# Input layer of batches 1 to 3 as seven half-size products, gated by Silu in one stretch per batch, and twelve output pairs

## The chip, the core and the metric

The kernel runs on one core of a Trainium2 chip, in one launch. The core's engines work from queues of their own and hand over by semaphores: TensorE (PE) multiplies and writes PSUM, VectorE (DVE) and ScalarE (ACT) read PSUM and SBUF, GpSimd (POOL) works in SBUF, SyncE (SP) issues most DMAs. The metric is the device time of one execution, in microseconds; lower is better.

## What is computed

Attention over 4 batches of 8 heads, 768 tokens and 64 dimensions, in which a query sees only the keys that the centroids assign to its own cluster, then two layers with a gate over 3072 tokens (512 to 2048 to 512).

```python
q_assign = np.argmax(np.einsum('bhsd,hcd->bhsc', q_n, c_n), axis=-1)
k_assign = np.argmax(np.einsum('bhsd,hcd->bhsc', k_n, c_n), axis=-1)
mask = q_assign[:, :, :, None] == k_assign[:, :, None, :]
scores = np.where(mask, scale * np.matmul(q, k.transpose(0, 1, 3, 2)), -1000000000.0)
...
attn = attn / (np.sum(attn, axis=-1, keepdims=True) + 1e-09)
x = np.matmul(attn, v).transpose(0, 2, 1, 3).reshape(B * S, H * D)
h = x @ w_in
g = h * (1.0 / (1.0 + np.exp(-h)))
out = g @ w_out
```

## The kernel before

Every instruction's place is set by hand: `plan` is a list of words, each word is one step, and each engine runs its share of the steps in that order. A word is an operation, a number, and where needed an engine (A for ACT, P for POOL, D for DVE) or a PSUM bank (0 to 3).

*Attention.* A job (`k0` to `k7`, `x0`, `x1`, `h8` to `h31`) is a head's query and key tiles: loaded (`r`), split into two fp16 parts (`hi`, `lo`), transposed (`tr`, `ht`). `L` or `l` multiplies them with the centroids (24 narrow matmuls or 12 wider ones, then `ls`, a sum on DVE); `mx` and `ge` make one-hot rows, which go back beside the tiles (`ct`, `cm`, `ce`; for later jobs `cs`, `cx`, `cv`) so that the score matmul masks itself. A unit is a head, a half of the tokens and 256 keys; there are 192. `qk` makes its scores (two matmuls of 384 columns into a PSUM tile of two banks, L325), `ex` their exponentials (L330), `pv` multiplies those of two heads with the values (36 matmuls of 65 columns, L342), `nm` divides (L352, L354), and `pt`, `pe` or `xd` put the transposed result into `xt`, a tile for each batch and token half.

*Input layer and gate.* For a batch, a token half and a block of 128 of the 2048 features, `e` (with `a`) multiplies four blocks of `w_in` with `xt` (four matmuls of 384 columns, L390). `t` takes tanh(h/2) on ACT (L402), `g` forms (tanh + 1) h on DVE (L405) into `gt`. There are 128 such units, and their words stand spread between the words of the attention of the next batch. One factor 0.5 is applied at the end.

*Output layer.* The six token tiles of a batch form three pairs, (0, 1), (2, 5) and (3, 4). A pair does the two-by-two product of half blocks with seven products (`m1` to `m7`, eight matmuls of 256 columns each, L477) in place of eight: `S1` to `S4` are sums of `gt` on DVE (L490) into `gt` itself or into three tiles, `wc` sums of `w_out` made once, and `z` and `o` take partial results out of PSUM (L499, L505, L508). In `m127` the pair is 12 and the product 7. The pair (0, 1) of batch 0 is left out: its tiles are plain products, `b` (16 matmuls of 512 columns each, L417), with `bo`. The output goes in rows of 512 columns, in the last batch in halves.

The order runs like this: the jobs and attention of batch 0, its input layer beside the attention of batch 1, its output pairs beside that too, and so on; at the end the input layer and the pairs of batch 3. PSUM has eight banks: four by name, and two tiles of two banks each for the scores.

Of the kernel before, what the change touches and what calls it, by code (L numbers as in the profile page):

```python
# [29 lines left out]
def kernel(  # L30
# [42 lines left out]
    zz = const.tile([128, 512], f16, name="zz")  # L73
# [52 lines left out]
    def tr(job, banks, parts="kq"):  # L126
        hl = hls[job.name]
        if job.name not in abs_:
            abs_[job.name] = mp.tile([128, 12, 128], f16, name="ab", bufs=12)
# [43 lines left out]

    def ohv(job):
# [13 lines left out]
    def ge_n(job):  # L188
        m = (job.n + 1) // 2
        nn[job.name] = len(nn)  # L190
# [15 lines left out]
    def c_xpose(job):  # L206
        cd = cds[job.name] = mp.tile([128, 2, 128], f16, name="cdt", bufs=4)
# [52 lines left out]
    vts, vns = {}, {}  # L260

    def load_v(i, eng=nc.sync):
        vn = mp.tile([128, NJ, D], f32, name="vn", bufs=5)
# [3 lines left out]
    def cast_v(i, eng=None):  # L267
# [5 lines left out]
        vts[i] = vt  # L273

# [53 lines left out]
    def exp(u):  # L328
        P = mp.tile([128, 2, HALF], f16, name="P", bufs=13)
# [46 lines left out]
    def xn_d(i, c):  # L376
        b = i // H
        if (b, c) not in xts:
            xts[b, c] = mp.tile([128, NR, HALF], f16, name="xt", bufs=3)
# [20 lines left out]
    def tanh(b, c, fb):  # L400
        tn = tns[b, c, fb] = mp.tile([128, HALF], f32, name="tn", bufs=3)
        nc.scalar.activation(out=tn, in_=phs[b, c, fb][:, 0:HALF], func=AF.Tanh, bias=0.0, scale=0.5)  # L402
# [7 lines left out]
    pos = {}  # L410

    def part_b(b, c, t, n, bk):
        if n == 0:
            pos[b, c, t] = bank("po", bk)
        po = pos[b, c, t]
# [3 lines left out]
    def part_out(b, c, t):  # L419
        j = c * NM + t  # L420
        ot = mp.tile([128, DM], f32, name="ot", bufs=4)
# [408 lines left out]
```

## Time and profile before

| What | Value |
| --- | --- |
| median of 3 runs | 298.83 us |
| lowest and highest | 298.75 and 300.07 us |
| profiled execution, first to last instruction | 297.9 us |
| matmuls of the input layer (L390) | 512, 96.1 us busy |
| matmuls of the output pairs (L477) | 616 |
| exp on ACT (L330) | 192, 151.0 us busy |
| tanh on ACT (L402) | 128, 61.6 us busy |
| gate on DVE (L405) | 128, 68.2 us busy |
| table loads on ACT | 1 |

The page gives the profiled execution by its span alone. In it, "busy" is the time in which at least one instruction of the engine or group ran; matmuls overlap each other, so the busy time of a group of them is more than its share of PE's time.

### The profile page before, as it was taken

How to read it: one execution, taken by the hardware profiler on the slowest of the kernel's cores; microseconds unless marked ns; L12 is line 12 of the kernel's file. 1: busy time of each engine (PE TensorE's matmuls, PEld its weight loads, DVE VectorE, ACT ScalarE, POOL GpSimd, SP SyncE). 2: the span in 40 equal slices, each digit the busy share in tenths (PEclk: the TensorE clock that was granted, in tenths of full speed). 3: DMA queues.
4: the chain of work that ended last, by engine and by line, in shares of the span. 5: the costliest groups of instructions: out<-in, count | busy, mean ns of one | idle time of the engine just before them, and what ended most of it. 6: DMA issues, size and time to landing. Idle time of an engine off the chain costs nothing.

```text
span 297.9 us, 8577 instructions
## 1 busy us (share of the span) xinstructions
PE 288.7 (97%) x3433; PEld 212.6 (71%) x3433; DVE 223.8 (75%) x489; ACT 233.2 (78%) x406; POOL 68.7 (23%) x124
## 2 busy tenths in 40 slices
PE   7899999999979999999999999999999999999995
PEld 3767766666658887777866887767867886777684
DVE  5898849689979986989467897788656733666663
ACT  5998999965979878999789876898669768964731
POOL 2655804000227001334444024220420000000000
PEclk9999999999999999999999999999999999999999
DMA  6999999999997899795399535867221102211103
GB/s 214 286 256 247 179 201 176 193 247 216 171 300 178 171 176 257 176 151 131 102 202 213 164 66 114 256 165 113 51 89 35 26 2 74 82 29 35 39 19 125
DMA packets 75208, 44.13 MB, mean 148 GB/s; under 512 B 54288, under 2 KB 70960, under 8 KB 75168
## 3 DMA queue, kind: packets, MB, share of 16 engines
q1 hardware_dynamic: 70272, 35.75, 50.3%
q0 software_dynamic: 4608, 7.54, 13.5%
q8 instruction: 27, 0.44, 0.6%
q10 hardware_dynamic: 288, 0.30, 0.3%
q14 instruction: 13, 0.11, 0.1%
HBM read 27.30 MB, written 6.29 MB: 113 GB/s over the span
## 4 chain that ended last, share of the span: by engine, by line
PE 87%; DMA 5%; ACT 3%; DVE 3%; issue 1%; SPq 0%; ACTq 0%
PE ph L390 25%; PE pS L325 20%; PE xb L477 18%; PE pO L342 12%; PE psN L159 4%; PE yb L477 3%; PE po L417 2%; DMA ab<-cd 2%; DMA ab<-hl 1%; DMA raw<-in_q_dram 1%; DVE hl L112 1%; PE wb L477 1%; ACT P L330 1%; ACT hl L103 1%; PE pTq L135 1%
## 5 line engine op out<-in xcount | busy, mean ns | idle before, releaser
L330 ACT ACTIVATE P<-pS 128x768 f16<-128x768 f32 x192 | 151.0, 815 | 18.8 <-PE pS L325 17.4
L390 PE MATMUL ph<-xt,win_s 128*128 128x384 f16 x512 | 96.1, 326 | 0.0
L405 DVE SCALAR_TENSOR_TENSOR gt<-tn,ph 128x384 f16<-128x384 f32 x128 | 68.2, 549 | 31.9 <-ACT tn L402 31.0
L325 PE MATMUL pS<-ab 128*128 128x384 f16 x384 | 86.7, 326 | 2.2 <-DMA ab<-cd 1.6
L402 ACT ACTIVATE tn<-ph 128x384 f32<-128x384 f32 x128 | 61.6, 499 | 13.9 <-PE ph L390 10.5
L390 PEld LDWEIGHTS <-win_s 128*128 128x128 f16 x512 | 49.4, 98 | 31.0 <-issue 0.3
L325 PEld LDWEIGHTS <-ab 128*128 128x128 f16 x384 | 34.2, 98 | 18.3 <-DMA ab<-cd 2.2
L342 PEld LDWEIGHTS <-P 128*128 128x128 f16 x1152 | 39.8, 97 | 3.8 <-DVE cd L234 0.4
L342 PE MATMUL pO<-vt,P 128*128 128x65 f16 x1152 | 41.2, 193 | 0.0
L477 PEld LDWEIGHTS <-gt 128*128 128x128 f16 x352 | 34.1, 98 | 6.5
L112 DVE SCALAR_TENSOR_TENSOR hl<-raw,hl 128x768 f16<-128x768 f32 (+3 forms) x35 | 32.0, 916 | 0.8 <-ACT hl L103 0.5
L105 POOL TENSOR_SCALAR hl<-raw 128x768 f16<-128x768 f32 (+1 forms) x9 | 19.5, 2167 | 47.2 <-DVE gt L405 30.7
L477 PEld LDWEIGHTS <-s 128*128 128x128 f16 x264 | 25.5, 98 | 4.7
L199 POOL TENSOR_SCALAR od<-od 128x96 f16<-128x96 f16 x16 | 8.4, 526 | 63.3 <-DVE od L192 63.2
L499 ACT ACTIVATE ot<-xb 128x256 f32<-128x256 f32 x33 | 12.7, 385 | 12.9 <-PE xb L477 12.6
L477 PE MATMUL xb<-wout_s,gt 128*128 128x256 f16 x176 | 22.6, 273 | 0.0
L159 PEld LDWEIGHTS <-ab 128*128 128x128 f16 x544 | 18.9, 97 | 4.1 <-DMA ab<-hl 0.5
L477 PE MATMUL xb<-wc,s 128*128 128x256 f16 x160 | 20.7, 272 | 0.0
L159 PE MATMUL psN<-stk,ab 128*128 128x16 f16 (+1 forms) x544 | 20.1, 184 | 0.1
L354 DVE TENSOR_TENSOR xn<-pO,zr 128x384 f16<-128x384 f32 x32 | 17.8, 557 | 1.1
L490 DVE TENSOR_TENSOR s<-gt 128x1024 f16<-128x1024 f16 x22 | 15.5, 712 | 1.3 <-PE xb L477 1.0
L212 POOL DMA_DIRECT2D ab<-cdt x16 | 9.0, 564 | 19.8 <-PE pS L325 5.2
(93 smaller groups left out, 258.2 us busy)
## 6 DMA issues: line engine op xcount, KB each, us to landing
raw<-in_k_dram SPq DMA_DIRECT2D x31, 192.0 KB, 3.9
raw<-in_q_dram SPq DMA_DIRECT2D x24, 192.0 KB, 3.5
out_dram<-ot SPq DMA_DIRECT2D x18, 256.0 KB, 2.9
vn<-in_v_dram SPq DMA_DIRECT2D x19, 192.0 KB, 4.7
vn<-in_v_dram POOLq DMA_DIRECT2D x13, 192.0 KB, 3.4
win_s<-in_moe_w_in_dram POOLq DMA_DIRECT2D x8, 256.0 KB, 6.8
wout_s<-in_moe_w_out_dram POOLq DMA_DIRECT2D x4, 512.0 KB, 9.2
out_dram<-ot SPq DMA_DIRECT2D x12, 128.0 KB, 1.8
```

The costliest lines, as they stand in the source:

```text
L105: nc.gpsimd.tensor_scalar(out=o, in0=i, scalar1=QS, scalar2=None, op0=ALU.mult)
L112: nc.vector.scalar_tensor_tensor(out=hl[:, s, 1, :], in0=raws[job.name][:, s, :], scalar=QS, in1=hl[:, s, 0, :], op0=ALU.mult, op1=ALU.sub ...
L159: nc.tensor.matmul(L[:, n % 2, :, n // 2], ab[:, i, :], stk[:, job.groups[i // 3][0], x : x + w], start=(x == 0), stop=(x + w == 2 * HC),)
L325: nc.tensor.matmul(pS[:, e, 0:HALF], abs_[kj.name][:, kn, :], rhs, start=True, stop=True)
L330: nc.scalar.activation(out=P, in_=pst.pop(u)[:, :, 0:HALF], func=AF.Exp, bias=0.0, scale=ESC)
L342: nc.tensor.matmul(o[:, (2 * t + h) * VW : (2 * t + h + 1) * VW], Ps[i + h, c, j // 2][:, j % 2, ts(t, 128)], vtb[(i + h) % 13][:, j, 0:VW ...
L354: nc.vector.tensor_tensor(out=xn, in0=ov[:, :, 0:D], in1=zr.unsqueeze(2).to_broadcast([128, 2 * NM, D]), op=ALU.mult)
L390: nc.tensor.matmul(ph[:, 0:HALF], win_s[:, r, ts(fb, 128)], xts[b, c][:, r, :], start=(r == 0), stop=(r == NR - 1))
L402: nc.scalar.activation(out=tn, in_=phs[b, c, fb][:, 0:HALF], func=AF.Tanh, bias=0.0, scale=0.5)
L405: nc.vector.scalar_tensor_tensor(out=gt[:, fb, NM * c : NM * c + NM, :].rearrange("p t n -> p (t n)"), in0=tns.pop((b, c, fb)), scalar=1.0 ...
L477: nc.tensor.matmul(o, self.lhs(l, f), self.rhs(r, f), start=(f == 0 and opens), stop=(f == HB - 1), skip_group_check=True)
L490: nc.vector.tensor_tensor(out=o, in0=a, in1=b_, op=op)
```

## The change

*Input layer of batches 1 to 3.* The two-by-two product is used here as well: the blocks are the two halves of the 512 inputs, the two halves of the 2048 features and the two halves of the tokens. A group `g` of eight covers 128 features of each half. `y` is one of its seven products (two matmuls of 384 columns), with the number batch, group, product: `y107` is batch 1, group 2, product 7. `ws` makes the sums of `w_in` once, `T` the sums of `xt` for each batch. Products 7, 2 and 4 add up in one bank (`gy`, or one half of `gd`), products 1, 6, 3 and 5 in another (`gx`, or the other half). Between the products the partial sums are joined: `u0` copies the bank of product 7 to `sb`, `u1` copies the bank of product 1 into it, `u2` and `u3` add `sb`. `s0` to `s3` are the gates of the four blocks, each one Silu on ACT into `gt`. Batch 0 keeps `e`, `t` and `g`.

*Stretches.* The words of a batch's input layer stand together, with few others between them, and the 48 units of the next batch come behind. One exp, `ex102`, stands within the first stretch.

*Output.* Pair (0, 1) of batch 0 is `Pair` number 11, so there are twelve pairs and no plain tiles. The values' column of ones is 2.0, which halves x; with that the factor 0.5 at the end and in the tanh goes, and Silu takes a scale of 2. Sums `S2` and `S4` go into `gt` in place, one tile `s3` is left, sums can be on POOL, copies from PSUM on DVE or ACT. Each half row is stored by itself.

*Places.* Score tiles have fixed banks (`d4`, `d5`), which the groups use as well. Some pools are smaller, `zz` lies in `s3`, `ohm` in `ohd`. Jobs 8, 10, 11 and 14 use `l` where they had `L`. The units' order within a batch is another one.

```diff
@@
-    ohm = [const.tile([128, 2 * HC * 6], f16, name=f"om{n}") for n in range(3)]
     ohd = [const.tile([128, 2, 128], f16, name=f"od{n}") for n in range(3)]
+    ohm = [t.rearrange("p h n -> p (h n)")[:, 0 : 2 * HC * 6] for t in ohd]
...
-            abs_[job.name] = mp.tile([128, 12, 128], f16, name="ab", bufs=12)
+            abs_[job.name] = mp.tile([128, 12, 128], f16, name="ab", bufs=10)
...
-        cd = mp.tile([6 * HC, 256], f16, name="cd", bufs=4)
+        cd = mp.tile([6 * HC, 256], f16, name="cd", bufs=3)
...
-    def qk_mm(u):
-        if u >= NU:
-            return
+    def double(name, n):
+        return ps.tile([128, 2, 512], f32, name=name, tag=f"d{n}", bufs=1)
+
+    def qk_mm(u, bk):
         i, c, m = units[u]
-        pS = ps.tile([128, 2, 512], f32, name="pS", tag="st", bufs=2)
+        pS = double("pS", bk)
...
-        P = mp.tile([128, 2, HALF], f16, name="P", bufs=13)
+        P = mp.tile([128, 2, HALF], f16, name="P", bufs=12)
...
-            xts[b, c] = mp.tile([128, NR, HALF], f16, name="xt", bufs=3)
+            xts[b, c] = mp.tile([128, NR, HALF], f16, name="xt", bufs=2)
...
-        tn = tns[b, c, fb] = mp.tile([128, HALF], f32, name="tn", bufs=3)
-        nc.scalar.activation(out=tn, in_=phs[b, c, fb][:, 0:HALF], func=AF.Tanh, bias=0.0, scale=0.5)
+        tn = tns[b, c, fb] = mp.tile([128, HALF], f32, name="tn", tag="tn", bufs=5)
+        nc.scalar.activation(out=tn, in_=phs[b, c, fb][:, 0:HALF], func=AF.Tanh, bias=0.0, scale=1.0)
...
-    def part_b(b, c, t, n, bk):
...
-        for fc in range(4 * n, 4 * n + 4):
-            nc.tensor.matmul(po, gt[:, fc, NM * c + t, :], wout_s[:, fc, :], start=(fc == 0), stop=(fc == NFB - 1))
...
+    def w_sum(g, k, eng):
+        s2, s3_, s4 = (ws[:, n, :, 256 * g : 256 * g + 256] for n in range(3))
+        o, a, b_, op = (
+            (s3_, w_half(0, 0, g), w_half(1, 0, g), ALU.subtract),
+            (w_half(1, 0, g), w_half(1, 0, g), w_half(1, 1, g), ALU.add),
+            (s2, w_half(1, 0, g), w_half(0, 0, g), ALU.subtract),
+            (s4, w_half(0, 1, g), s2, ALU.subtract),
+        )[k]
+        eng.tensor_tensor(out=o, in0=a, in1=b_, op=op)
...
+    def x_sum(b, k, eng):
...
+            (t3, x_half(b, 1, 1), x_half(b, 0, 1), ALU.subtract),
+            (x_half(b, 0, 1), x_half(b, 0, 1), x_half(b, 0, 0), ALU.subtract),
+            (t2, x_half(b, 1, 1), x_half(b, 0, 1), ALU.subtract),
+            (t4, x_half(b, 1, 0), t2, ALU.subtract),
...
+    def group_mm(b, g, s, bk):
+        if s in (7, 1):
+            if s == 7 and bk > 3:
+                o = double("gd", bk)
+                ys[b, g, 7], ys[b, g, 1] = o[:, 0, :], o[:, 1, :]
+            elif (b, g, s) not in ys:
+                ys[b, g, s] = bank("gy" if s == 7 else "gx", bk)
+        o = ys[b, g, 7 if s in (7, 2, 4) else 1]
...
+        for r in range(2):
+            nc.tensor.matmul(
+                o[:, 0:HALF], w[:, r, :], x[:, r, :], start=(s in (7, 1) and r == 0), stop=(r == 1), skip_group_check=True
+            )
+
+    def group_mix(b, g, k, eng):
+        y = ys[b, g, 7][:, 0:HALF]
+        if k == 0:
+            sbs[b, g] = mp.tile([128, HALF], f32, name="sb", tag="tn", bufs=5)
+        sb = sbs[b, g]
+        if k < 2:
+            o, i = (y, ys[b, g, 1][:, 0:HALF]) if k else (sb, y)
+            if eng == "D":
+                nc.vector.tensor_copy(o, i)
+            else:
+                nc.scalar.activation(out=o, in_=i, func=AF.Copy, bias=0.0, scale=1.0)
+        else:
+            x = ys[b, g, 1][:, 0:HALF]
+            nc.vector.tensor_tensor(out=(y, sb)[k - 2], in0=x, in1=sb, op=ALU.add)
...
+    def group_silu(b, g, j):
+        i, o = group_h(b, g, j)
+        nc.scalar.activation(out=o, in_=i, func=AF.Silu, bias=0.0, scale=2.0)
...
-                "S3": (sums["S3"], a11, a21, ALU.subtract),
+                "S3": (s3, a11, a21, ALU.subtract),
                 "S1": (a21, a21, a22, ALU.add),
-                "S2": (sums["S2"], a21, a11, ALU.subtract),
-                "S4": (sums["S4"], a12, sums["S2"], ALU.subtract),
+                "S2": (a11, a21, a11, ALU.subtract),
+                "S4": (a12, a12, a11, ALU.subtract),
             }[name]
-            nc.vector.tensor_tensor(out=o, in0=a, in1=b_, op=op)
+            eng.tensor_tensor(out=o, in0=a, in1=b_, op=op)
...
-    duos = [Pair(b, x, y) for b in range(B) for x, y in ((0, 1), (2, 5), (3, 4)) if (b, x) != (0, 0)]
+    duos = [Pair(b, x, y) for b in range(B) for x, y in ((0, 1), (2, 5), (3, 4)) if (b, x) != (0, 0)] + [Pair(0, 0, 1)]
...
+        o2 m114 ls21 qk97.5 ex100 o1.D mx21 qk96.4 l22.3 o112 ex97 y101.0 ge21 ex96 v21.P T10.D T11.D y81.1 y107.2
+        y97.5 y117.4 ls22 y87.3 u100.A u101.A u90.D ws2.P T12.P u110.A y91 y102 s100 y111 y106 u80.D u81.D y82 cs21
+        u91.D y92 y96 T13.D s80 y86 u111.D y112 y116 u102 y105 u82 vl31 y85 s90 u92 cv20 u103 ws3.P s110 cx19 u112
```

ACT in the input layer of batch 1, before: exponentials (`P`) of batch 2 and tanh (`tn`) take turns, with copies out of a pair (`ot`).

```order
L330 ACTIVATE P<-pS 128x768 x2
L402 ACTIVATE tn<-ph 128x384
L330 ACTIVATE P<-pS 128x768
L402 ACTIVATE tn<-ph 128x384
L330 ACTIVATE P<-pS 128x768
L402 ACTIVATE tn<-ph 128x384
L330 ACTIVATE P<-pS 128x768
L402 ACTIVATE tn<-ph 128x384 x2
```

ACT at the start of the first stretch, in the changed program: the last exponentials, three copies (`u`), then a load of the table, and Silu (into `gt`) from the banks and from `sb`.

```order
L338 ACTIVATE P<-pS 128x768 x6
L481 ACTIVATE sb<-gy 128x384
L481 ACTIVATE gy<-gx 128x384
L481 ACTIVATE sb<-gd 128x384
L494 ACT_TABLE_LOAD
L494 ACTIVATE gt<-gy 128x384 x2
L494 ACTIVATE gt<-gd 128x384 x2
L102 ACTIVATE hl<-raw 128x12x64
```

Further on in that stretch, on ACT, at `ex102`:

```order
L494 ACTIVATE gt<-gd 128x384 x2
L494 ACTIVATE gt<-gy 128x384 x2
L338 ACT_TABLE_LOAD
L338 ACTIVATE P<-pS 128x768
L494 ACT_TABLE_LOAD
L494 ACTIVATE gt<-gy 128x384 x2
```

Exponentials and gate no longer alternate; where they do change, a load stands between them. There are eight loads where there was one.

DVE in the input layer of batch 1, before: gates (`gt` from `tn` and `ph`) among the sums, maxima and one-hot rows of the jobs and the divisions of the attention.

```order
L405 SCALAR_TENSOR_TENSOR gt<-tn,ph 128x384
L192 TENSOR_TENSOR od_92<-L,mxn 128x2x96
L405 SCALAR_TENSOR_TENSOR gt<-tn,ph 128x384 x2
L352 RECIPROCAL zr<-pO 128x6
L354 TENSOR_TENSOR xn<-pO,zr 128x384
L192 TENSOR_TENSOR od_93<-L,mxn 128x2x96
L405 SCALAR_TENSOR_TENSOR gt<-tn,ph 128x384
```

DVE in the first stretch, in the changed program: sums of `xt` (`T`), then copies and additions of partial sums (`u`), almost by themselves.

```order
L447 TENSOR_TENSOR tx<-xt,tx 128x768
L479 COPY gd<-gd 128x384
L484 TENSOR_TENSOR gy<-gx,sb 128x384 x2
L484 TENSOR_TENSOR gd<-gd,sb 128x384
L484 TENSOR_TENSOR sb<-gx,sb 128x384
L484 TENSOR_TENSOR gd<-gd,sb 128x384
L111 SCALAR_TENSOR_TENSOR hl<-raw,hl 128x12x64
L484 TENSOR_TENSOR sb<-gx,sb 128x384
```

The gates are gone from DVE there, and about as many steps on partial sums have come in.

POOL at the first three output pairs, in the changed program: sums for a pair (`s_93` is the tile `s3`) behind casts of values (`vt`), a sum for `ws`, and a `hi` (`hl`).

```order
L278 CAST vt_75<-vn 128x6x64
L564 TENSOR_TENSOR s_93<-gt 128x1024
L278 CAST vt_79<-vn 128x6x64
L432 TENSOR_TENSOR win_s<-win_s 128x2x256
L104 TENSOR_SCALAR hl<-raw 128x12x64
L564 TENSOR_TENSOR s_93<-gt 128x1024
L564 TENSOR_TENSOR gt<-gt 128x8x128
L737 MEMSET od_88 128x256
L564 TENSOR_TENSOR gt<-gt 128x8x128 x2
```

Before, all sums of the pairs stood on DVE (L490); POOL had none.

More of the change, by code (lines that the diff above doesn't have):

```diff
@@ L172, in lsum @@
         Ls[job.name] = L[:, :, :, 0:m]
+    turn = """
+        k0 k1 k2 k3 k4 k5 k6 k7 x0 x1 h8 h10 h9 h11 h12 h13 h14 h15
+        h16 h17 h18 h20 h19 h21 h22 h23 h24 h26 h25 h27 h28 h29 h30 h31
+    """.split()
     def ohv(job):
@@ L257, in ct_k @@
             )
[L260 removed]
+    vts, vns, vn_slot = {}, {}, {}
+    vn_free = list(range(5))
     def load_v(i, eng=nc.sync):
[L263 removed]
+        vn_slot[i] = vn_free.pop(0)
+        vn = mp.tile([128, NJ, D], f32, name="vn", tag=f"vn{vn_slot[i]}", bufs=1)
         eng.dma_start(vn.rearrange("p j d -> p (j d)"), v[i // H, i % H].rearrange("(p j) d -> p (j d)", j=NJ))
@@ L504, in out @@
             if (r, c) == (0, 1):
-                nc.scalar.activation(out=o, in_=self.xb[:, 0:DH], func=AF.Copy, bias=0.0, scale=0.5)
+                self.copy(o, eng)
             else:
                 i = self.yb[:, 0:DH] if r == 0 else self.wb[:, DH:DM]
-                nc.vector.scalar_tensor_tensor(out=o, in0=i, scalar=0.5, in1=o, op0=ALU.mult, op1=ALU.add)
-            self.ot[r][1] += 1
+                nc.vector.tensor_tensor(out=o, in0=i, in1=o, op=ALU.add)
             rows = out[self.b * S : (self.b + 1) * S, :].rearrange("(p j) d -> p j d", j=NJ)[:, t, :]
-            if self.b == B - 1:
-                nc.sync.dma_start(rows[:, c * DH : c * DH + DH], o)
-            elif self.ot[r][1] == 2:
-                nc.sync.dma_start(rows, self.ot[r][0])
-    sums = {n: mp.tile([128, HB, 128], f16, name=n.lower()) for n in ("S2", "S3", "S4")}
+            nc.sync.dma_start(rows[:, c * DH : c * DH + DH], o)
+    s3 = mp.tile([128, HB, 128], f16, name="s3")
     done_exp = []
```

250 lines of the change are left out of this document (146 added, 104 removed).

## The prediction

> **What bounds the kernel now.** I read the busy shares on the page first, then the busy time by stretch, then the list of TensorE's (PE's) waits, longest in total first.
>
> ```profile
> span 297.9 us, 8577 instructions
> PE 288.7 (97%) x3433; PEld 212.6 (71%) x3433; DVE 223.8 (75%) x489; ACT 233.2 (78%) x406; POOL 68.7 (23%) x124
> ```
>
> ```profile
> 120.00:284.00 164.00, 164.00 (x1823) 121.82 (x1819) 117.84 (x245) 129.53 (x232) 31.49 (x59) 1.00 0.45 105
> ```
>
> ```profile
> PE pS L325 <- DMA ab<-cd: 1.6, 1, 1.6
> ```
>
> The second fence is one stretch: its length, the busy time of PE, its weight loads, DVE, ACT and POOL, then the granted clock. PE is busy 164.00 of 164 us, at the full clock, while DVE has 28% free and ACT 21%; in the third, its largest wait (in total, times, longest) is 1.6 us, once. So the time is the sum of PE's instructions, and a matmul less is time won, as long as PE still waits for nobody. A busy share can hide slack inside, so I also take the step from one matmul to the next:
>
> ```profile
> 221.21 1.46 PE L390 MATMUL ph<-xt,win_s 128*128 128x384 f16 x8
> 222.51 0.49 PE L325 MATMUL pS<-ab 128*128 128x384 f16 x2
> ...
> 223.49 0.68 PE L342 MATMUL pO<-vt,P 128*128 128x65 f16 x17
> ...
> 283.78 1.04 PE L477 MATMUL yb<-wout_s,gt 128*128 128x256 f16 x8
> 284.65 1.04 PE L477 MATMUL xb<-wout_s,gt 128*128 128x256 f16 x8
> ...
> 71.90 0.76 PE L159 MATMUL psN<-stk,ab 128*128 128x16 f16 x24
> 72.50 1.46 PE L390 MATMUL ph<-xt,win_s 128*128 128x384 f16 x8
> ...
> 74.83 0.52 PE L159 MATMUL psN<-stk,ab 128*128 128x32 f16 x12
> 75.19 0.98 PE L390 MATMUL ph<-xt,win_s 128*128 128x384 f16 x5
> ```
>
> In these lines of the timeline (start, length, engine, line, what, count) from start to start: eight matmuls of 384 columns in 1.30 us, so 0.1625 each; eight of 256 in 0.87, so 0.109 each. Seventeen of 65 take 0.68, one 0.193 (the page's mean), so they step by 0.03 and a set of 36 (`pv`) takes 1.1. A logits set of 24 narrow matmuls takes 0.60 us, one of 12 wider ones 0.36.
>
> **What PE loses.** The input layer of a batch was 2 x 16 x 4 = 128 matmuls of 384 columns; seven products of two matmuls over eight groups are 112. Three batches: 48 fewer x 0.1625 = **7.8 us**. In the output layer the two tiles of batch 0 that were plain (32 matmuls of 512 columns, twice the 0.109: 7.0 us) become a twelfth pair (56 x 0.109 = 6.1): **0.9 us**. Four jobs (h8, h10, h11, h14) go from L to l: 4 x 0.24 = **1.0 us**. The floor moves by 9.7 us.
>
> **What may come back.** Within a stretch nothing but input-layer work, and little else, feeds PE, so the other two engines must keep up with 112 x 0.1625 = 18.2 us.
>
> ```profile
> L330 ACT ACTIVATE P<-pS 128x768 f16<-128x768 f32 x192 | 151.0, 815 | 18.8 <-PE pS L325 17.4
> ...
> L402 ACT ACTIVATE tn<-ph 128x384 f32<-128x384 f32 x128 | 61.6, 499 | 13.9 <-PE ph L390 10.5 <-DVE mxn L183 2.0
> L559 ACT ACT_TABLE_LOAD x1 | 1.3, 1283 | 1.7 <-PEq L814 1.7
> ...
> 105.19 1.50 ACT L330 ACTIVATE P<-pS 128x768 f16<-128x768 f32 x2
> 121.86 0.87 ACT L402 ACTIVATE tn<-ph 128x384 f32<-128x384 f32 x2
> ...
> L405 DVE SCALAR_TENSOR_TENSOR gt<-tn,ph 128x384 f16<-128x384 f32 x128 | 68.2, 549 | 31.9 <-ACT tn L402 31.0
> L112 DVE SCALAR_TENSOR_TENSOR hl<-raw,hl 128x768 f16<-128x768 f32 x26 | 25.4, 979 | 0.1
> ...
> 200.99 1.02 DVE L405 SCALAR_TENSOR_TENSOR gt<-tn,ph 128x384 f16<-128x384 f32 x2
> ```
>
> Back to back, a tanh steps by 0.87 - 0.499 = 0.37 us, a gate by 1.02 - 0.549 = 0.47, an exp by 0.69 (two in 1.50, one alone 0.815). Silu is not in the trace; one ACT row of the same shape is the tanh, and the exp at twice the width bounds it above, so I take 0.37. The copies and additions of partial sums are as wide as a gate: 0.47 on DVE, 0.37 on ACT. In the first stretch ACT then has 35 x 0.37, a `hi` and an exp (as wide as each other, 0.7 each) and three loads (3.8): 18.2 us; in the others 15 to 16.5. DVE has 29 x 0.47 = 13.6, two `lo` (2.0) and three sums of x tiles (as wide as a gate in their fp16 pairs, 1.5 to 2): 17.4. Both fit under PE's 18.2 plus the 2 to 3 us of other PE work inside, the first stretch with least to spare. So DVE's edit (96 gates out, 79 partial-sum steps in) I cost at nothing, covered by PE; without the cover it is the last rival. A lighter DVE or ACT can't give time back either, since PE waits for neither.
>
> *Start of a stretch.* The chain to PE is: product 7 (a pair, 0.49), copy, copy (0.50 each), one more copy (0.37), the table load (1.28), Silu (0.50), addition (0.55), and six hand-overs. A hand-over is 0.03 to 0.04:
>
> ```profile
> 289.02 1.04 PE L477 MATMUL xb<-wout_s,s 128*128 128x256 f16 x8
> ...
> 290.09 0.38 ACT L505 ACTIVATE ot<-xb 128x256 f32<-128x256 f32 x1 [0.49 <-PE xb L477]
> ...
> 290.51 0.42 DVE L508 SCALAR_TENSOR_TENSOR ot<-xb,ot 128x256 f32<-128x256 f32 x1 [2.61 <-ACT ot L505]
> ```
>
> Together that is 4.4 us from the start of product 7 to the first product 5, which stands in PE's order behind 14 products, that one included. So it fits by 0.1 us (14 x 0.325 = 4.55). Between nothing and a whole load (1.28) I take half, 0.7, for three starts: **2.1 us**.
>
> *The exp inside the first stretch.* ex102 takes a load before and after it: 3.25 us without a Silu. Behind it PE has eleven products and one score pair, 3.9 us, before pv16 wants the bank that the next Silu frees. Between 0 and two loads (2.6) I take **0.6**. At the end of a stretch the load back is hidden by pair products (3 x 6.1 us); without them it would cost 1.3 each.
>
> *Sums on POOL.* 21 of the 48 S sums stand on POOL, and `m17`, `m16` and `m6` stand close behind theirs. On DVE such a sum takes 0.71 us; POOL made none before, and its nearest rows are the last two:
>
> ```profile
> L490 DVE TENSOR_TENSOR s<-gt 128x1024 f16<-128x1024 f16 x22 | 15.5, 712 | 1.3 <-PE xb L477 1.0
> ...
> L105 POOL TENSOR_SCALAR hl<-raw 128x768 f16<-128x768 f32 x6 | 14.2, 2374 | 41.7 <-DVE gt L405 30.7 <-DMA raw<-in_k_dram 10.9
> L272 POOL CAST vt<-vn 128x384 f16<-128x384 f32 x15 | 8.1, 547 | 8.5 <-PE pO L342 5.9 <-DMA vn<-in_v_dram 2.1 <-DMA raw<-in_k_dram 0.5
> ```
>
> Per element that is 1.42 ns (cast) to 3.09 (scale), so 1024 take 1.5 to 3.2 us. S13 may only start when m7 has read the one `s3`; from there to m17 PE's order holds 5.7 us of work, and POOL's a cast, a sum for `ws`, a `hi` and S13: 5.1 to 7.7. From m17 to m16 it is 4.6 us against 3.3 to 6.7 (S11, a memset, S12), from m16 to m6 1.2 against 1.5 to 3.2. Waits together 0.3 to 6.0 us. An add of fp16 tiles is nearer to the cast, since it has no scale, but reads two tiles; at 2.2 us a sum the three waits are 0.4, 0.1 and 1.0: **1.5 us**.
>
> Smaller pools (xt 2, P 12, ab 10, cd 3) and 48 stores of 128 KB for 30 stores I cost at 0; the price of a pool that binds once would be like the 1.6 us wait above.
>
> **Sum.** 9.7 - 2.1 - 0.6 - 1.5 = 5.5 us off the profiled 297.9 (the span is the profiled execution's own time here; no other is listed): 292.4. The median of the runs is 298.83, 0.9 above that span, so **293.3**.
>
> **Rivals.**
> *All of it is hidden.* PE waits as little as now: 298.8 - 9.7 = 289.1. For it: no wait of PE is over 1.6 us in 298 now, though ACT is busy 78% and DVE 75%. Against: three starts with 0.1 us to spare. Chance 0.16.
> *The switch costs twice the load row.* If ACT must first run empty, a switch costs like two loads, 2.57. Each start then waits 1.3 (3.9), ex102 2.6: 6.5 in place of 2.7, so 297.1. The one load in the trace comes before any work on ACT and can't show it. The Trainium skill ("ScalarE: Activation LUTs", What ACT_TABLE_LOAD costs) has 1283 ns for the load, with which the trace agrees, and 1380 ns more for the drain, 2.66 in all. Chance 0.12.
> *POOL at the upper row.* A POOL row stretches beside DVE:
>
> ```profile
> L105 POOL TENSOR_SCALAR hl<-raw x9: 1642/2142/3051, 8.3 to 158.2; 128x768 f16<-128x768 f32 x6, 128x576 f16<-128x576 f32 x3
> ```
>
> Shortest, median and longest: the same work takes up to 3.05 us. At 3.2 us a sum the waits are 6.0 in place of 1.5: 297.8. The Trainium skill ("GPSIMD Engine Reference", Specifications) says that POOL's SBUF interface is shared with VectorE, with contention when a VectorE instruction has two SBUF inputs, as the sums left on DVE have; the spread of that row agrees. Chance 0.10.
> *The stretch is bound by latency, and it is slower than before.* A group holds two of the eight PSUM banks from product 7 to its last Silu, so four groups run at once and a stretch is two rounds; a round may last 9.1 us. From the rows the chain is 4 matmuls (0.82), copy, copy, pair, Silu, add, pair, add, pair, Silu with nine hand-overs: 5.8 us. Six of its steps stand on ACT and DVE, whose queues run in order and are near full here. If each stands behind one other instruction of 0.5 us the chain is 8.8 and still costs nothing. From 10.4 on (0.8 behind each step) two rounds in each of three stretches take 6 x 1.3 = 7.8 us, and the time passes 300; at 11 it is 6 x 1.9 = 11.4 us, less 1 us of it that is in the sum already: 303.7. For it: every partial-sum step needs the one before it on another engine. Against it: the steps of four groups interleave, and DVE's 17.4 us and ACT's 15 to 18 leave it some room. Chance 0.16.
>
> **How the numbers follow.** The forecast (290.5 to 296) has 0.46. What a measurement can tell from no change here is 0.5%, 1.5 us: 297.3 to 300.3. Faster: 0.46 + 0.16, half of the switch's 0.12 and 0.02 of POOL's: 0.70. Same: 0.06 + 0.08 = 0.14. Slower: 0.16. The range goes from just under the floor, 288.8, to 299.0, which takes in both upper bounds one at a time and leaves out the latency rival.
>
> **What would show it.** Matmul steps of 0.1625 us in the y products, 336 of them; seven more ACT_TABLE_LOAD of about 1283 ns, and what ACT does just ahead and behind; PE's waits by releaser: under 1 us for a stretch start on ACT or DVE, about 1.5 us on POOL's s3 and gt near m17, m16, m6. A stretch of 19 to 22 us from its first to its last product is right; 24 or more is the latency rival. POOL rows of 1024 over 2.4 us, or y products that wait over 2 us in each round, make the prediction wrong.

## The result, and the profile after

| | before | after |
| --- | --- | --- |
| median | 298.79 us (4 runs, 298.67 to 300.07) | 322.14 us (4 runs, 318.91 to 325.12) |
| ratio, 95% interval | | 1.073 (1.068 to 1.079): slower |
| span of the profiled execution | 297.9 us | 320.5 us |

Ratios, here and below, are of the executions in the faster of the two states that the core shows, medians of all of them. The forecast was 293.3 us with a range of 288.8 to 299.0, and 0.70 for faster. It was wrong, and on the wrong side. First the head of the page of the changed kernel: busy time, share of the span and instructions of each engine.

```profile
span 320.5 us, 8556 instructions
PE 289.4 (90%) x3361; PEld 209.2 (65%) x3361; DVE 242.6 (76%) x496; ACT 243.1 (76%) x405; POOL 142.0 (44%) x166
```

PE now idles 31.1 us of the span, where it idled 9.2. The matmuls did become fewer: 464 + 384 of 384 columns against 896, 672 of 256 in place of 616 and 32 of 512. With the steps of the prediction I summed, over all records, the step that each matmul needs, and apart from it what lies between its start and the next start beyond that step. The first sum fell from 282.0 to 272.4 us, by 9.6. The second, PE's waits and slow steps, rose from 10.9 to 43.3. By place, with three of the experiments below (their program is up to 17 us ahead in the later rows):

| us of the span | before | after | e7 | e8 | e10 |
| --- | --- | --- | --- | --- | --- |
| 0 to 20 | 5.7 | 5.6 | 5.8 | 5.8 | 5.5 |
| 20 to 80 | 3.1 | 7.8 | 7.4 | 6.1 | 6.4 |
| 80 to 120 | 1.9 | 10.5 | 3.0 | 2.7 | 3.0 |
| 120 to 160 | 0.0 | 8.5 | 9.0 | 5.6 | 4.5 |
| 160 to 200 | 0.0 | 2.4 | 1.8 | 2.6 | 2.3 |
| 200 to 220 | 0.0 | 4.4 | 0.4 | 0.6 | 0.6 |
| 220 to the end | 0.1 | 4.1 | 7.4 | 6.9 | 3.9 |
| sum | 10.9 | 43.3 | 34.8 | 30.4 | 26.2 |

Two places stand out in the second column: 80 to 120 us, the end of batch 0, and the starts of the stretches of batches 1 and 2, near 140 and 212. The list of PE's waits (in total, times, longest) names whom it waited for:

```profile
PE psC L225 <- DVE od L196: 4.4, 3, 1.9
PE gy L467 <- DVE tx L447: 4.3, 1, 4.3
PE gd L467 <- DVE tx L447: 2.5, 1, 2.5
PE xb L551 <- DVE ot L573: 1.8, 1, 1.8
PE pO L350 <- DVE ot L587: 1.6, 1, 1.6
PE pO L350 <- DVE cd L238: 1.3, 1, 1.3
```

All six name DVE, none POOL or ACT. What DVE was doing shows the busy time by window (PE, weight loads, DVE, ACT, POOL, granted clock), first in the kernel before, then in the changed one:

```profile
80.00:100.00 20.00, 18.43 (x229) 14.14 (x228) 18.31 (x40) 17.00 (x29) 9.38 (x11) 1.00 0.91 239
```

```profile
80.00:100.00 20.00, 13.35 (x145) 9.64 (x144) 19.83 (x29) 11.52 (x21) 12.95 (x9) 1.00 0.69 154
100.00:120.00 20.00, 17.75 (x239) 14.15 (x237) 19.56 (x35) 15.46 (x25) 12.98 (x13) 1.00 0.71 169
140.00:160.00 20.00, 15.28 (x81) 8.15 (x80) 14.48 (x28) 12.10 (x24) 12.40 (x15) 0.91 0.57 164
```

At the end of batch 0 DVE is full with only 29 instructions in 20 us, where 40 took 18.3 us before. They are not more, they are longer. The timeline of both engines there:

```profile
86.89 2.11 POOL L564 TENSOR_TENSOR s<-gt 128x1024 f16<-128x1024 f16 x1
86.97 2.24 DVE L196 TENSOR_TENSOR od<-L,mxn 128x192 f16<-128x192 f32 x1
...
89.07 2.12 POOL L564 TENSOR_TENSOR gt<-gt 128x1024 f16<-128x1024 f16 x1
89.14 2.33 DVE L514 TENSOR_TENSOR wc<-wc,wout_s 128x512 f16<-128x512 f16 x1
```

The group of the same `od` in the kernel before:

```profile
L192 DVE TENSOR_TENSOR od<-L,mxn 128x192 f16<-128x192 f32 x16 | 5.6, 351 | 0.2
```

The `od` takes 351 ns on average there, the `wc` 416. Here each begins just behind a POOL sum and ends just after that sum: 89.07 + 2.12 = 91.19, against 91.47. DVE isn't slowed by a share, it is held. Over the program, DVE's time above the shortest time of each of its forms (its excess) is 32.9 us, where it was 12.1; 16.8 of it are in instructions that run beside POOL's pair sums. The Trainium skill ("SBUF — State Buffer", 🔬 SBUF: two separate sides) describes it so: the port pair that the two engines share is an exclusive lock for a whole instruction, and the other one blocks fully. These rows agree, with 2.2 us for a sum as the price.

The start of the first stretch, first on PE, then on DVE, both from the timeline:

```profile
139.82 0.81 PE L467 MATMUL gx<-xt,win_s 128*128 128x384 f16 x4
144.90 0.80 PE L467 MATMUL gy<-tx,ws 128*128 128x384 f16 x2 [4.26 <-DVE tx L447]
145.49 1.49 PE L467 MATMUL gd<-tx,ws 128*128 128x384 f16 x4
```

```profile
134.40 0.56 DVE L362 TENSOR_TENSOR xn<-pO,zr 128x384 f16<-128x384 f32 x1
...
144.29 0.56 DVE L447 TENSOR_TENSOR tx<-xt 128x768 f16<-128x768 f16 x1 [4.12 <-DMA xt<-xn]
```

The first operand sum T10 waits for the DMA transpose of the last pair (`xd15`). Its source `xn` was ready at 134.96; 9.3 us pass until T10. The queue of SP tells why (start, time to issue):

```profile
135.77 1.50 SPq L212 DMA_TRANSPOSE cdt<-od  x1
137.37 0.89 SPq L589 DMA_DIRECT2D out_dram<-ot  x1
138.35 1.18 SPq L389 DMA_TRANSPOSE xt<-xn  x1
139.58 0.56 SPq L91 DMA_DIRECT2D raw<-in_q_dram  x1
140.20 0.42 SPq L91 DMA_DIRECT2D raw<-in_k_dram  x1
140.72 0.38 SPq L589 DMA_DIRECT2D out_dram<-ot  x1
141.19 1.20 SPq L389 DMA_TRANSPOSE xt<-xn  x1
```

It issues without a pause, so the transpose starts 6.2 us after its data was there, and lands 3 us later. Of the 6.2 us ahead of it the two stores take 1.3; the rest are transposes and loads. At the second stretch it is 6.3 us from `xn` to T20. Behind such a wait PE is also slow. At the second stretch:

```profile
214.89 0.82 PE L467 MATMUL gd<-tx,ws 128*128 128x384 f16 x4 [2.51 <-DVE tx L447]
215.55 1.20 PE L467 MATMUL gy<-tx,ws 128*128 128x384 f16 x4
216.54 0.85 PE L467 MATMUL gd<-xt,win_s 128*128 128x384 f16 x2
217.18 0.85 PE L467 MATMUL gx<-xt,win_s 128*128 128x384 f16 x2
```

From 216.54 on two matmuls take 0.64 us, twice the 0.325 of full speed, until 219.1. In the same stretch of time the granted clock reads 0.50; before the wait it reads 1.00. At the first stretch the four from 145.49 take 1.28 for 0.65, at a granted clock of 0.50 too.

The first wait stands in the profile of every version that keeps these transposes and stores, with 4.0 to 4.8 us (in e12 it falls to idle matmuls). The second does not. These are the only lines for `tx` in the lists of e6, e7 and e14, three of the experiments below, in that order:

```profile
PE gy L467 <- DVE tx L447: 4.0, 1, 4.0
```

```profile
PE gy L467 <- DVE tx L447: 4.6, 1, 4.6
```

```profile
PE gy L467 <- DVE tx L447: 4.6, 1, 4.6
```

They, and e2 and e3, have the same order of SP at the second stretch, but T20 comes 2.8 to 3.1 us behind `xn` there, and PE loses 0.1 to 0.5 us from 200 to 220 us, not 4.4. In the profile of the changed kernel two transposes shortly before took SP 5.4 us to issue (3.2 in e6), and the last one began 1.8 us later than in e6. So the loss at the second start comes and goes with the execution, and only the first is a fixed part of the order.

### The profile page after: what moved, and what is told of

Read it like the earlier page. It is cut to its first block, busy times and chain, and to the rows that moved or that the text cites. A ratio compares the mean times of both kernels' runs of the same rounds, so it can differ in the third digit from the quotient of the medians.

```text
span 320.5 us, 8556 instructions
## 1 busy us (share of the span) xinstructions
PE 289.4 (90%) x3361; PEld 209.2 (65%) x3361; DVE 242.6 (76%) x496; ACT 243.1 (76%) x405; POOL 142.0 (44%) x166
## 4 chain that ended last, share of the span: by engine, by line
PE 44%; DVE 23%; ACT 11%; DMA 9%; issue 7%; SPq 2%; POOL 1%; POOLq 1%; DVEq 0%; ACTq 0%
PE xb L551 10%; PE pS L333 9%; PE pO L350 8%; ACT P L338 7%; PE gd L467 6%; DVE hl L111 4%; PE gx L467 4%; PE gy L467 3%; DVE gt L413 3%; DMA ab<-cd 3%; DVE wc L514 2%; DVE L L167 2%; DMA ab<-hl 2%; DVE hl L106 2%; DVE gt L564 1%
## 5 line engine op out<-in xcount | busy, mean ns | idle before, releaser
L551 PEld LDWEIGHTS <-gt 128*128 128x128 f16 x576 | 55.8, 98 | 15.9 <-issue 3.7
L551 PE MATMUL xb<-wout_s,gt 128*128 128x256 f16 x288 | 37.1, 272 | 0.5 <-DVE L L167 0.4
L564 POOL TENSOR_TENSOR gt<-gt 128x1024 f16<-128x1024 f16 x13 | 28.7, 2208 | 7.8 <-PE psC L225 3.7
L564 POOL TENSOR_TENSOR s<-gt 128x1024 f16<-128x1024 f16 x8 | 17.0, 2124 | 31.2 <-ACT gt L494 22.2
L467 PEld LDWEIGHTS <-win_s 128*128 128x128 f16 x192 | 19.1, 100 | 16.0 <-issue 4.7
L467 PEld LDWEIGHTS <-ws 128*128 128x128 f16 x144 | 14.3, 101 | 17.2 <-issue 6.5
L551 PE MATMUL xb<-wc,gt 128*128 128x256 f16 x176 | 22.7, 272 | 2.3 <-DVE ot L573 1.8
L398 PE MATMUL ph<-xt,win_s 128*128 128x384 f16 x128 | 24.1, 326 | 0.0
L564 DVE TENSOR_TENSOR gt<-gt 128x1024 f16<-128x1024 f16 x23 | 20.0, 877 | 3.4 <-PE yb L551 2.2
L360 DVE RECIPROCAL zr<-pO 128x6 f32<-128x6 f32 x32 | 6.2, 192 | 21.2 <-PE pO L350 20.8
L278 POOL CAST vt<-vn 128x384 f16<-128x384 f32 x20 | 12.1, 615 | 22.2 <-DMA vn<-in_v_dram 14.3
L413 DVE SCALAR_TENSOR_TENSOR gt<-tn,ph 128x384 f16<-128x384 f32 x32 | 16.7, 546 | 4.2 <-ACT tn L410 4.1
```

Of the source, the lines that this page charges most:

```text
L278: (nc.vector if eng == "D" else nc.gpsimd).tensor_copy(vt[:, :, 0:D], vns.pop(i))
L398: nc.tensor.matmul(ph[:, 0:HALF], win_s[:, r, ts(fb, 128)], xts[b, c][:, r, :], start=(r == 0), stop=(r == NR - 1))
L413: nc.vector.scalar_tensor_tensor(out=gt[:, fb, NM * c : NM * c + NM, :].rearrange("p t n -> p (t n)"), in0=tns.pop((b, c, fb)), scalar=1.0 ...
L467: nc.tensor.matmul(o[:, 0:HALF], w[:, r, :], x[:, r, :], start=(s in (7, 1) and r == 0), stop=(r == 1), skip_group_check=True)
L551: nc.tensor.matmul(o, self.lhs(l, f), self.rhs(r, f), start=(f == 0 and opens), stop=(f == HB - 1), skip_group_check=True)
L564: eng.tensor_tensor(out=o, in0=a, in1=b_, op=op)
```

## The experiments

Theory A, the first I tried, was that POOL's sums hold DVE and that this is the whole loss. Its rivals were the order of the sums in DVE's queue, the transposes (theory Q, "queues"), and the table switches (theory B). Times are medians; the kernel before ran beside each set at 298.2 to 299.5. Each version has one profile.

**e1, e2, e3: sums moved from POOL to DVE, at the same places.**

```diff
-... ws0.P ...   S3.P m7 ...   T11.D y81.1 ... T12.P
+... ws0.D ...   S3.D m7 ...   T11.D y81.1 ... T12.D
```

e1 moves all of them, e2 the pair sums, e3 those of weights and x.

> The changed kernel with all 33 sums that stood on GpSimd (21 S, 8 ws, 4 T with their places kept) on VectorE. Theory A (a GpSimd sum of two tiles holds VectorE instructions that read two SBUF tiles until it ends, so VectorE is late and PE waits): VectorE rows wc, od, lo, hi are back at their short durations, PE's surplus of 43 us over its matmul steps falls to about 20, the time to about 300 (297 to 304). Rival B (the stretches and the table switches cost the time): over 314. Rival C (PE waits for the sums because one takes 2.1 us in place of 0.7, VectorE not being held): also falls, to about 305, but the long wc and od rows stay long.

> The changed kernel with only the 21 S sums on VectorE; ws and T stay on GpSimd. A: 16 of the 23 us that VectorE rows are stretched beside GpSimd sums are beside S sums, so most of the gain of the full move: about 304 (300 to 309). B: over 314. C: about as A.

> The changed kernel with only the ws and T sums on VectorE; the S sums stay on GpSimd. A: 3 of the 23 us go, so little: 319 (315 to 322). B: 322. If the wait of 4.3 us at the first stretch comes from the T sum on GpSimd itself: about 316.

Measured: e1 321.25 us (ratio 1.068 to 1.081), e2 320.77 (1.065 to 1.078), e3 319.35 (1.060 to 1.074), against 322.14 (1.068 to 1.079). DVE's excess fell as A says, in e1 to 12.5 us, but the time did not: e1 and e2 end where rival B put them, and e3, whose ranges overlap, doesn't tell A from B. In e1 PE waits for the sums themselves:

```profile
PE xb L551 <- DVE s L564: 4.8, 3, 3.0
PE gy L467 <- DVE tx L447: 4.2, 1, 4.2
PE xb L551 <- DVE gt L564: 3.3, 3, 1.2
```

S3 now stands at the end of a queue of DVE work that PE had outrun. Theory A as the whole cause falls; B is tested by e6.

**e4: the hold by itself.** The kernel before, with 32 POOL sums that nobody waits for, two behind every third exp of the end of batch 0. Each two stand behind a small copy on POOL that waits for that exp, so POOL's queue is held for that time as well.

```diff
+            nc.gpsimd.tensor_tensor(out=zz, in0=zz, in1=zz, op=ALU.subtract)
```

> The kernel before, with 32 sums of two fp16 tiles of 512 columns on GpSimd, two after every third exponential from ex42 to ex87. They add zeros in a tile that nobody reads, so nobody waits for their results. A: VectorE instructions with two SBUF tiles (wc, od, lo) that fall beside them grow to 1 to 2.4 us, PE waits for VectorE, and the time goes up by 3 to 12 us. C and B: at most 1 us, from casts and hi on GpSimd that start later.

Measured: 311.48 us, ratio 1.041 (1.036 to 1.046), so 12 us more. The group of these sums, and what PE waited for between 95 and 125 us, where before it waited for nobody:

```profile
L538 POOL TENSOR_TENSOR zz<-zz 128x512 f16<-128x512 f16 x32 | 36.3, 1134 | 1.3
```

```profile
PE psN L159 <- DVE ot L508: 2.2, 1, 2.2
PE xb L477 <- DVE wc L443: 2.1, 1, 2.1
PE pO L342 <- POOL vt L272: 2.1, 1, 2.1
```

DVE's excess rose from 12.1 to 23.8 us, 13.9 of it beside these sums. So the hold is real; but one wait of the three is for a cast in POOL's own, now longer, queue, and behind the other two PE ran at a granted clock of 0.5 for 3.4 us each. How much of the 12 us the hold alone makes isn't separated.

**e11: the same with one-input products by 1.**

```diff
-            nc.gpsimd.tensor_tensor(out=zz, in0=zz, in1=zz, op=ALU.subtract)
+            nc.gpsimd.tensor_scalar(out=zz, in0=zz, scalar1=1.0, scalar2=None, op0=ALU.mult)
```

> The kernel before with 32 idle products by one on POOL (128x512, one input) at the places where e4_before_idle_sums had 32 idle two-input sums; nobody waits for the results. Theory A2 (only the two-input form holds VectorE): under 3 us slower than before, 298 to 302 us, VectorE's time over its own minimum near 12 us. Rival (any work of POOL on SBUF of that length holds it): 308 to 313 us, as e4_before_idle_sums.

Measured: 313.14 us (1.043 to 1.051), as slow as e4, so the expectation on the time fails. The mechanism is another one: DVE's excess is 15.6 us, only 6.0 of it beside these products, though they keep POOL busy for 50 us. DVE and PE wait for POOL's queue instead, in which a `hi` now stands late (waits of DVE, then of PE, 95 to 125 us):

```profile
DVE hl L112 <- POOL hl L105: 9.0, 1, 9.0
...
PE xb L477 <- DVE wout_s L443: 9.4, 1, 9.4
```

Both ways of loading POOL cost, by different paths.

**e5: the last two pairs of batches 1 and 2 turned by PE, not by DMA.**

```diff
-nm14 xd14 qk93.4 l20.3 r24 ...            nm15 xd15 m3 ... l23.3 ls23 qk99.5
+nm14 qk93.4 l20.3 pt14.0 pe14.D r24 ...   nm15 m3 ... l23.3 ls23 pt15.0 pe15.D qk99.5
```

> The changed kernel, but the last two pairs of the later token half of batches 1 and 2 (xd14, xd15, xd22, xd23) are turned by TensorE and copied by VectorE, as the kernel does it for batch 3, instead of by DMA transposes. Theory Q (the time is lost in waits at a few places, each a late item in an in-order queue; at the starts of stretches 1 and 2 it is the DMA transpose, which stands behind a dozen issues on SP): the two waits of 4.3 and 2.5 us go, and with them the slow matmuls that follow (2 to 3.5 us): 312 to 316 us, granted clock 1.00 in both places. Theory R (the stretch cannot start earlier anyway, since the operand sums on VectorE and POOL and the first copies are what is late): under 2 us gained, 320 to 323, and PE still waits for tx.

Measured: 318.98 us (314.25 to 320.64, ratio 1.048 to 1.066). In the profiled run, the fastest of the four, both waits are gone, with the slow steps behind them:

```profile
140.29 0.81 PE L467 MATMUL gx<-xt,win_s 128*128 128x384 f16 x4
140.94 0.49 PE L467 MATMUL gy<-tx,ws 128*128 128x384 f16 x2
141.26 0.81 PE L467 MATMUL gd<-tx,ws 128*128 128x384 f16 x4
```

From first to last product the first stretch lasts 22.5 us (28.1 in the changed kernel), the second 21.1 (25.4). What PE loses in the first fell from 7.5 to 1.8, and a new wait of PE for `xn` ahead of the turns takes 1.1 back. In the second it fell from 4.9 to 0.6, but e6, e7 and e14 have 20.8 to 21.2 us there without this edit, so that fall can't be put down to it; a new wait of 0.8 comes with it. The median fell by 3 us, and by the ratios, 1.057 in place of 1.073, it is 5: short of the 6 to 10 expected. The span of the profiled run fell by 8.0, but against a profile that has the second wait. Theory Q holds at the first stretch.

**e6: no table switch.** `AF.Silu` becomes `AF.Tanh` in the stretches.

> The changed kernel, but the gate of batches 1 to 3 applies Tanh where it applied Silu, so that ScalarE never loads a second table (the gate computes another function). Theory Q: ScalarE is not what is late at the starts; the seven loads of 1.28 us lie in ScalarE's waits for TensorE but for some 2 us: 319 to 322 us. Theory B (the switches of the table cost more than their 1.28 us and set the stretches): 312 to 317 us.

With it the gate is another function, so this version computes something else. Measured: 320.82 us (1.062 to 1.075), not to be told from the changed kernel. The first stretch lasts 27.9 us, as with the loads. The second lasts 20.8, but with the loads in place it is 21.2 in e7 and 21.1 in e14. Theory B falls.

**e7 and e14: the sums of batch 0 ahead in the order, on DVE and on POOL.**

```diff
-mx12 e26.0 wc8 ge12 g25 ... ge13 S3.P m7 ... wc15 S13.P cm15.2 ... wc14 S12.P ... S2.P
+mx12 e26.0 wc8 ge12 S3.D g25 ... ge13 m7 ... ge15 S13.D ... o10 S12.D ... nm9 S2.D
```

In e7 all 33 sums are on DVE, as in e1; in e14 they are on POOL, as in the changed kernel. Both also move five sums of weights behind these, and `hi17`, `hi18` and `z10` from DVE to ACT.

> The changed kernel, with all two-input sums on VectorE (as in e1_all_sums_dve), and those of batch 0's output pairs moved ahead in the plan to where their operands are ready: S3 from behind ge13 to behind ge12, S13 from behind wc15 to behind ge15, S12 ahead of wc14, S2 ahead of wc2 and wc11; five weight sums moved behind them; hi17, hi18 and z10 on ScalarE. Theory Q (in e1 the sums stood late in VectorE's queue; POOL's sums hold VectorE in the kernel as changed): of e1's 321 us go the waits for S3 (3 to 3.5 us), the slow matmuls behind (2 us) and about 3 us of waits for the others: 311 to 316 us, no wait over 1.5 us between 80 and 112 us. Theory W (VectorE has too much work there, whatever the order): 319 to 322 us.

> e7_early_sums, but the sums that the changed kernel has on POOL are on POOL again, at the early places. If what costs at 80 to 112 us is the place of the sums in the order alone (theory O): as e7, 313 to 316 us. If POOL's sums cost by holding VectorE (theory A), wherever they stand: 318 to 323 us, VectorE's time over its own minimum again some 30 us.

Measured: e7 314.89 us (1.048 to 1.055), e14 317.82 (1.059 to 1.070). e14 lies 4.3 us below the changed kernel, but the two intervals overlap a little, and e7 2.9 below e14. The profiles say more. Between 20 and 120 us PE loses 18 us in the changed kernel, 19 in e1 (DVE, late), 18 in e14 (POOL, early) and 10 in e7 (DVE, early, as in the table): neither the place nor the engine alone wins there, both together win 8. On the other side e7, like e1, loses 7.4 us from 220 us on, where the changed kernel loses 4.1 and e14 3.9, so there the sums stood better on POOL. The time of e14 ends just below the range of A, and well above that of O. In e14 DVE is held as before, its excess 32.3 us:

```profile
93.99 2.37 POOL L564 TENSOR_TENSOR gt<-gt 128x1024 f16<-128x1024 f16 x1
...
94.31 2.27 DVE L196 TENSOR_TENSOR od<-L,mxn 128x192 f16<-128x192 f32 x1
...
96.63 0.31 PE L225 MATMUL psC<-ident,od 128*96 128x128 f16 x2 [2.11 <-DVE od L196]
```

In e7 the same window has PE at 18.89 of 20 us, where it was 13.35.

```profile
80.00:100.00 20.00, 18.89 (x250) 14.34 (x248) 19.46 (x42) 18.19 (x30) 4.21 (x6) 1.00 1.05 213
```

**e8: e5 and e7 together, and `cd` with four buffers.**

> e5_pe_turn and e7_early_sums together, and the fourth buffer of cd given back (the changed kernel has three; VectorE waits 1.6 us there for the DMA that reads one). Theory Q: the savings add, and 1 to 2 us for cd: 300 to 308 us. Theory R or W: where one of the two gains nothing, 311 to 318 us; if both, 319 or more.

Measured: 310.23 us (1.034 to 1.041), 11.9 below the changed kernel. The savings in the medians add, but end 2 us above the range that Q gave. The wait of PE for `cd` (1.3 us) is gone.

**e9: stores of batches 0 to 2 issued by ACT.**

```diff
-            nc.sync.dma_start(rows[:, c * DH : c * DH + DH], o)
+            (nc.scalar if self.b < B - 1 else nc.sync).dma_start(rows[:, c * DH : c * DH + DH], o)
```

> The changed kernel, but the stores of the output pairs of batches 0 to 2 are issued from ScalarE's queue, not from SP's. Theory P (SP's queue is what makes the DMA transposes late: it issued 24 stores of half rows more in these batches, and was issuing for 18 to 20 of 20 us where the kernel is late): the wait for tx at the first stretch falls from 4.3 us to under 1.5 and at the second from 2.5 to under 1; 314 to 319 us, less what ScalarE loses by issuing. Theory D (the transposes are late because of their own slot in the plan, just behind their normalisation): the wait at the first stretch stays over 3 us, 321 to 325.

In batches 0 to 2 these are 36 half rows, where the kernel before had 18 whole ones (18 more, not the 24 that the expectation names). Measured: 335.94 us (1.115 to 1.126). ACT runs in order, so an exp behind a store waits for the DVE result that is stored; the group of exps has 18.4 us of such idle time ahead of it:

```profile
L338 ACT ACTIVATE P<-pS 128x768 f16<-128x768 f32 x192 | 147.4, 812 | 50.0 <-PE pS L333 21.5 <-DVE ot L587 18.4 <-DVE L L167 3.0
```

As a version it fails. As a measurement of SP's queue it is of use: from the end of the last `xn` (149.14) to T10 (153.44) it is now 4.3 us instead of 9.3, and PE waits 0.2 us for `tx` there. How much of this is the stores' own, and how much the slower pace that leaves SP more time, it doesn't separate; the two stores that stood ahead of the transpose account for 1.3 us. At the second stretch it is 3.1 us, as in the versions that leave the stores alone.

**e12: idle matmuls in the two waits.** `j20.3` ahead of the first product with tx of batch 1, `j11.2` ahead of that of batch 2 (20 and 11 matmuls of 512 columns).

> The changed kernel with matmuls whose result nobody reads put into the two waits for tx (20 of 512 columns ahead of the first product with tx of batch 1, 11 ahead of that of batch 2). Theory K (the slow matmuls behind these waits are the price of the wait itself, by the granted clock): the wait stays, the clock stays at 1.00 in both windows, the products behind step by 0.16 us a matmul from the first on: 2 to 5 us gained, 317 to 320. Rival: the slow steps have another cause (late operands, PSUM) and stay: 321 to 325.

Measured: 327.95 us (1.091 to 1.100). At the first stretch it failed as an experiment: the idle matmuls took a bank that `ls22` frees, and DVE runs `ls22` behind T10, so they began only after the wait. At the second they ran without a gap:

```profile
219.10 2.54 PE L613 MATMUL junk<-s 128*128 128x512 f16 x11
221.48 0.81 PE L467 MATMUL gd<-tx,ws 128*128 128x384 f16 x4
```

Every product behind steps by 0.1625 us. But T20 ended at 220.03 in this profile, so without them PE would have waited for 1 us, not 2.5: there was hardly a wait to fill, and e12 doesn't show K. What speaks for K is the granted clock itself, 0.50 over just the slow steps of the changed kernel, and that e6, e7 and e14, without the wait, have no slow step at that place. The time missed the 317 to 320 of K and the 321 to 325 of its rival, since the failed half costs 6 us.

**e10 and e13: small moves at the waits that e8 shows.**

```diff
-S61.D qk160.4 ... S62.D m66 ...   pv23.1 ... qk145.5 pt23.1
+S61.D S62.D qk160.4 ... m66 ...   pv23.1 ... qk145.5 ex145 ... qk148.4 pt23.1
```

> e8_both with eight small moves in the plan, each at a wait that its trace shows: S62 right behind S61 (1.3 us), S91 and S92 ahead of S103 and four copies of the last pairs on ScalarE (1.7 us), three turns by TensorE one score product later (0.9 us each), l21 two score products later (0.6 us). Theory Q: what remains of the loss are small waits that the plan causes, so each move wins its wait: 303 to 307 us. Rival C (waits are conserved: the next one takes the place, since another engine sets the pace): 309 to 311 us.

> e10_tuned with its order mended (there S91 stood ahead of the gate that writes its second operand, so that its output was not the reference's), and more moves of the same kind: weight sums of both layers taken from 60 to 80 us, where VectorE is busy for 19.7 of 20 us, to 110 to 140; four copies of turned rows on ScalarE; ls22 ahead of the second operand sum T11; S22 right behind S21. Theory Q: each move wins its wait, some 3 to 4 us below e10_tuned's 306: 301 to 304 us. Rival C (the next wait takes the place): 305 to 308 us.

Measured: e10 306.09 us (1.019 to 1.026), in the range expected. But e10 puts S91 ahead of the gate that writes its second operand, so it computes something else. e13, with that mended, took 307.04 (1.023 to 1.034), no further: Q's 301 to 304 fails, and rival C's 305 to 308 holds. About 3 us of what e10 gains over e8 lie from 220 us on (3.9 lost for 6.9), and e13 keeps them. In e13 DVE is relieved between 60 and 80 us, from 19.7 to 18.2 of 20, and PE still doesn't gain there. No version of the changed kernel came below the kernel before.

## Why the prediction was wrong

**The floor was right.** 9.7 us fewer of PE's own work were forecast, 9.6 came.

**"Start of a stretch", 2.1 us, is the first step that failed.** It timed the chain from product 7 through copies and the table load, and took the operands of product 7 as ready. The loads are there, seven of 1283 ns, and none sets the time (e6). What was late is the operand: T10 waits for the last DMA transpose. The wait of 4.3 us and the slow steps in and behind it made the first stretch lose 7.5 us, and with the transposes taken out (e5) it lost 1.8. In this profile the second stretch lost 4.9 us in the same way, but five versions with the same order there lost next to nothing, so that part is the execution's own. The prediction cost the new stores at 0 and did not look at SP's queue at this place, where the transpose stands 6.2 us behind its data; the stores are 1.3 us of that, the rest are transposes and loads. The order of SP should have been read up to T10, and for each DMA ahead its issue time taken, 0.4 us for a store and 1.2 for a transpose.

**"Sums on POOL", 1.5 us: the duration was right, the payer wrong.** 2.2 us a sum were forecast, 2.21 and 2.12 measured on average, single ones up to 2.78. But PE's waits at m17, m16 and m6 don't name POOL. The cost came through DVE, which the prediction had at nothing in "DVE's edit I cost at nothing, covered by PE". That cover was read from 120 to 284 us, where DVE had 28% free; from 60 to 100 us it had little, with 18.4 and 18.3 of 20 us busy already before. The rival on POOL used the sharing of the interface to make POOL slower, and never asked whether DVE stands still. (In that rival's row the shortest time, 1642 ns, is of a narrower tile; the tiles of 768 columns take 2.13 to 3.05 us.) Between 80 and 120 us PE lost 8.6 us more than before. e7 takes 7.2 us off the time by the early order and DVE together; neither change alone removes the loss there (e1, e14).

**"Smaller pools at 0"**: one did bind. `cd` with three buffers cost PE a wait of 1.3 us, close to the price that the prediction named for such a case; in e8 it is gone. `xt` and `P` show no such wait. SP's waits for PE ahead of the transposes into `ab` rose from 14.8 to 23.5 us, and PE waited once for such a transpose, 0.9 us; no run takes this apart.

**The rivals.** *The switch costs twice* is refuted by e6, and by the rows in the section on the hardware. *The latency rival* had the right sign for a wrong reason. Its own mark, a stretch of 24 us or more, did appear (28.1, 25.4, 25.3), but e5 brings the first to 22.5 by its start alone, the second is 20.8 to 21.2 wherever T20 comes in time, and the third has only 1.3 us of waits: it is long because output products of batch 3 stand in it. The mark didn't tell the two apart.

**What stays open.** From the best version that computes the same, 307.0, to what the floor would allow, 298.8 - 9.6 = 289.2, there are 18 us. PE's waits beyond steps in e13 sum to 26.6 us against 10.9 before, most of them under 1 us and spread over the span. e10's moves won 4 us; e13 added more of the kind, and other waits took the place of those removed. DVE is busy about 19.2 of 20 us from 80 to 120 in e8, e10 and e13, so it may set the pace there, but no run takes more than a few short steps from it in that place, and between 60 and 80 us, where e13 does, PE gained nothing. This stays a guess. So more than half of what the kernel lost is not accounted for by an experiment. Nor is it known how often the wait at the second stretch comes: with one profile for each version, a difference of 4 to 5 us between two spans can be that wait alone.

## What to carry to other kernels

On a kernel with PE 97% busy, fewer matmuls are worth what they save only if every in-order queue that feeds PE still delivers in time: for each new first consumer, go through the queue of its producer, DMA issues included, and add up what stands ahead. A two-input sum moved to POOL is not off DVE's back, since DVE can stand still for its whole length; give it to POOL only where DVE idles. When a sum changes engines, its place in the order has to change with it (e1 won nothing, e7, with three more steps taken from DVE, 7 us). And a wait seen in one profile should be looked for in the profiles of other versions before an edit gets the credit for its end.

## What the hardware showed that I had not expected

- POOL's two-input sum of 128x1024 fp16 takes 2.1 to 2.2 us and holds a DVE instruction until it ends: 0.42 became 2.33 us. One-input rows of DVE were held too: a `hi` (fp32 to fp16, 0.55 us alone) took 2.48 us beside a sum of 2.78. A one-input product on POOL held DVE far less, 6.0 us of excess beside 50 us of products (e11) against 13.9 beside 36 us of sums (e4).
- A wait of PE of 2.5 us was enough for half speed, and it came 1 us after PE had gone on (a granted clock of 0.79 from 214.9 to 216.5 us, 0.50 to 219.1, 0.96 to 221). The Trainium skill ("TensorE: Matmul & The Clock Gate", 🎯 Why this matters for your kernels) warns of idle gaps over about 3 us; here a shorter one did it. The length alone doesn't decide: behind waits of 2.0 us (e1, at 27.7) and 2.8 (e6, at 101.2) the clock read 0.50 for 3.4 us, behind waits of 2.6 (e14, at 107.0), 2.7 (e12, at 102.4) and 3.1 (e9, at 140.6) it stayed at 1.00. Every wait of 4 us or more in these runs was followed by half speed. Two waits of 1.7 and 1.6 us, 1 us apart, left the clock at 1.00 in the changed kernel, and at 0.91 over 80 to 100 us in e5.
- A table load costs its 1283 ns and no more. In e8 it stands between two instructions that have no other reason to wait: copy, load and Silu follow each other at once.

```profile
133.71 0.49 ACT L481 ACTIVATE sb<-gd 128x384 f32<-128x384 f32 x1
134.22 1.28 ACT L494 ACT_TABLE_LOAD   x1
135.51 0.49 ACT L494 ACTIVATE gt<-gy 128x384 f16<-128x384 f32 x1
```

The gaps ahead of and behind the load are 0.02 us; the 1380 ns for a drain that one rival took from the Trainium skill ("ScalarE: Activation LUTs", What ACT_TABLE_LOAD costs) are not there.
